# The second group's x times w_a, w_b and w_in with seven block products in place of eight

## The chip, the core and the metric

The kernel runs on one core of a Trainium2 chip. TensorE (PE in the profile; PEld is its loading of weights) multiplies, VectorE (DVE), ScalarE (ACT) and GpSimd (POOL) do the rest on rows of up to 448 columns, SyncE (SP) issues the DMAs. TensorE alone writes products into PSUM, eight banks of 512 float32 columns; VectorE and ScalarE read them there, GpSimd works on SBUF only. The metric is the device time of one execution in microseconds, lower is better.

## What is computed

Attention with normalised q and k over 4 batches of 12 heads (448 tokens, 64 columns a head), then two feed-forward layers on the 1792 tokens of 768 columns. Cut to what matters:

```python
def rmsnorm(x, g):
    return x / np.sqrt(np.mean(x * x, axis=-1, keepdims=True) + 1e-06) * g
scores = scale * np.matmul(rmsnorm(q, g_q), rmsnorm(k, g_k).transpose(0, 1, 3, 2))
attn = np.exp(scores - np.max(scores, axis=-1, keepdims=True))
attn = attn / (np.sum(attn, axis=-1, keepdims=True) + 1e-09)
x = np.matmul(attn, v)                              # to (1792, 768)
x = ((x @ w_a) * (x @ w_b)) @ w_out                 # w_a, w_b: 768 x 1536
h = x @ w_in                                        # 768 x 2048
out = (h * np.clip(h + 3.0, 0.0, 6.0) / 6.0) @ w_out2
```

## The kernel before

Tokens stand in columns. A batch has 448, so one matmul has 448 columns and 128x128 of weights. Every operand of the feed-forward layers lies as two float32r parts, a high one (rounded by ScalarE) and a low one (the rest, by a subtraction on VectorE or GpSimd, `sub`, line 342), and a product is three matmuls: high x high, high x low, low x high (`tri`, lines 627 to 629).

The batches form two groups of two (`GB`). Attention of all four batches comes first in due time; the first group's layers run beside the attention of the later batches, and the second group's layers after that. The `layer` calls at lines 786 to 790 are: first layer for batch 0, for batch 1, second layer for both; then first and second layer for the second group. A weight piece is 128 rows of a product, 768 wide: it is converted once from the stored 64-bit form (`convert`) and kept in DRAM, and each later use loads it (`wf`), rounds it whole on ScalarE (line 612) and makes the low part in two halves of 384 columns (`piece`). In the second group the low parts are VectorE's alone (`no_pool`).

In a layer, `unit` makes 128 rows of x times w_b, w_a or w_in for one batch in one PSUM bank, 18 matmuls. VectorE gates (`up_a`, `up_i`), and the result is split into `act`. `down` takes two rows of chunks (`SLICE`) and adds w_out's product to `acc`: for each of 6 blocks of 128 output rows and each batch a bank with six matmuls, called a unit of `down` below, then an addition on VectorE (line 721). After the last `down` of the first layer `acc` is the next layer's x and is split into `xx` (`to_x2`, line 735); the second group's first x comes from attention in `xf` and is split by `next_x` while the first group's last `down` runs.

What stands where on each engine is decided beforehand: `Plan.run` takes every operation with its due time, its cost by engine and its needs, goes through time on paper, lets each free engine take the most urgent operation whose data and buffers are there, and emits the instructions in that order. The costs written at the operations (378 for two matmuls of scores, 1135 for six of a unit, 567 for three of `down`) and the due times (`T` for the heads of each batch, `R` for each layer pass) set the order. On the chip each engine works through its own row, and waits where an operand isn't there. PSUM banks and SBUF buffers are `Slot`s which `Buf`s take in turn, the first free one of a list.

## Time and profile before

| | |
|---|---|
| median of 3 runs | 1321.78 us (1321.41 to 1322.69) |
| profiled execution: span from the first to the last instruction | 1319.6 us |
| TensorE busy | 99% of the span |
| VectorE, ScalarE, GpSimd busy | 68%, 46%, 13% |

The profiled execution has no time of its own beside the span; the median of the runs is 2.2 us above it. A busy share tells how much of the span an engine worked, not whether it was waited for; the chain of waits follows the last instruction back to what released it each time. Busy shares by stretch show where the engines' loads differ: attention and the first group until some 810 us, the second group's layers alone from 820 us on. In rows of single instructions, start and duration are in us, and what ended an idle time stands in brackets. Matmuls overlap: one takes 0.37 us, and the next begins 0.2 us after it.

### The profile page before, as it was taken

The numbers are of one execution on the slowest core, as the hardware profiler recorded it, in microseconds if no ns is written. First come the engines' busy times: TensorE is split into PE (matmuls) and PEld (weight loads), VectorE is DVE, ScalarE is ACT, GpSimd is POOL, SyncE is SP. The second block draws the span as 40 slices with busy tenths as digits, with TensorE's granted clock in tenths as the row PEclk, the third lists the DMA queues.
The fourth block names the chain that finished last, engine by engine and source line by source line (L and its number), as shares of the span: only waits on it lengthen the run. The fifth ranks groups of instructions, "written<-read, shape, count | busy, mean of one in ns | idle before, by whom it ended". The sixth has DMA issues, their size and how long they took to land.

```text
span 1319.6 us, 17987 instructions
## 1 busy us (share of the span) xinstructions
PE 1302.0 (99%) x6648; PEld 1097.5 (83%) x6648; DVE 891.3 (68%) x1648; ACT 609.6 (46%) x1249; POOL 171.5 (13%) x228
## 2 busy tenths in 40 slices
PE   5999999999999999999999999999999999999998
PEld 3668888888888888888887887999999999999997
DVE  8998999876576898877778654445444454555554
ACT  6886767675244566547556652111111143222220
POOL 3423222330010220111111012000000030000000
PEclk8999999999999999999999999999999999999999
DMA  6446776664332554444334113221111111111102
GB/s 210 162 142 230 246 253 226 216 216 131 97 104 89 162 178 159 160 163 143 99 137 164 45 44 113 61 60 48 59 50 60 48 52 58 48 60 48 61 24 84
DMA packets 52361, 155.32 MB, mean 118 GB/s; under 512 B 5936, under 2 KB 18608, under 8 KB 52272
## 3 DMA queue, kind: packets, MB, share of 16 engines
q1 hardware_dynamic: 52272, 154.16, 35.4%
q8 instruction: 52, 0.85, 0.3%
q14 instruction: 37, 0.30, 0.1%
HBM read 121.90 MB, written 32.24 MB: 117 GB/s over the span
## 4 chain that ended last, share of the span: by engine, by line
PE 98%; DVE 1%; ACT 0%; DMA 0%; SPq 0%; issue 0%; POOL 0%; DVEq 0%; ACTq 0%
PE bank L627 26%; PE bank L629 25%; PE bank L628 25%; PE bank L543 7%; PE bank L516 5%; PE bank L478 3%; PE bank L479 3%; PE bank L443 1%; PE bank L530 1%; PE bank L532 1%; PE bank L554 0%; PE bank L533 0%; DMA gg<-in_g_dram 0%; ACT p L488 0%; DVE rn L430 0%
## 5 line engine op out<-in xcount | busy, mean ns | idle before, releaser
L627 PE MATMUL bank<-xx,w 128*128 128x448 f32 x960 | 359.1, 374 | 0.0
L629 PE MATMUL bank<-xx,w 128*128 128x448 f32 x960 | 352.3, 367 | 0.0
L628 PE MATMUL bank<-xx,w 128*128 128x448 f32 x960 | 352.2, 367 | 0.0
L612 ACT ACTIVATE w<-wf 128x768 fp32r<-128x768 f32 x172 | 141.8, 842 | 338.2 <-PE bank L628 329.8
L627 PE MATMUL bank<-act,w 128*128 128x448 f32 x672 | 252.0, 375 | 0.0
L721 DVE TENSOR_TENSOR acc<-bank,acc 128x448 f32<-128x448 f32 x264 | 164.3, 623 | 122.1 <-PE bank L629 120.1
L629 PE MATMUL bank<-act,w 128*128 128x448 f32 x672 | 246.7, 367 | 0.0
L628 PE MATMUL bank<-act,w 128*128 128x448 f32 x672 | 246.6, 367 | 0.0
L627 PEld LDWEIGHTS bank<-xx,w 128*128 128x128 f32 x960 | 180.3, 188 | 19.6 <-issue 1.4
L629 PEld LDWEIGHTS bank<-xx,w 128*128 128x128 f32 x960 | 180.2, 188 | 16.9
L628 PEld LDWEIGHTS bank<-xx,w 128*128 128x128 f32 x960 | 180.5, 188 | 15.5
L342 DVE TENSOR_TENSOR w<-wf,w 128x384 fp32r<-128x384 f32 x283 | 148.4, 567 | 37.4 <-ACT w L612 33.2
L627 PEld LDWEIGHTS bank<-act,w 128*128 128x128 f32 x672 | 126.2, 188 | 16.7 <-DVE acc L721 2.4
L629 PEld LDWEIGHTS bank<-act,w 128*128 128x128 f32 x672 | 126.2, 188 | 12.0
L628 PEld LDWEIGHTS bank<-act,w 128*128 128x128 f32 x672 | 126.3, 188 | 10.9
L484 DVE TENSOR_REDUCE nm<-bank 128x1 f32<-128x448 f32 x168 | 102.3, 619 | 29.4 <-PE bank L479 24.0
L353 ACT ACTIVATE pt<-bank 128x512 f32<-128x512 f32 (+1 forms) x127 | 69.5, 550 | 98.9 <-PE bank L516 92.0
L488 ACT ACTIVATE p<-bank,nm,rstd 128x448 f32<-128x448 f32 x133 | 95.6, 721 | 29.5 <-PE bank L532 20.4
L342 POOL TENSOR_TENSOR w<-wf,w 128x384 fp32r<-128x384 f32 x61 | 65.5, 1087 | 290.7 <-ACT w L612 266.4
L670 ACT ACTIVATE act<-bank 128x448 fp32r<-128x448 f32 x112 | 60.8, 543 | 87.5 <-DVE bank L688 43.9
L543 PE MATMUL bank<-pt,rv 128*64 128x448 f32 (+1 forms) x384 | 93.3, 567 | 0.0
L342 DVE TENSOR_TENSOR act<-bank,act 128x448 fp32r<-128x448 f32 x112 | 69.5, 621 | 29.2 <-ACT act L670 28.7
(93 smaller groups left out, 1393.7 us busy)
## 6 DMA issues: line engine op xcount, KB each, us to landing
wst<-in_w_dram SPq DMA_DIRECT2D x68, 768.0 KB, 5.0
wf<-kept SPq DMA_DIRECT2D x104, 384.0 KB, 3.1
kept<-wf SPq DMA_DIRECT2D x68, 384.0 KB, 2.6
rq<-in_qt_dram SPq DMA_DIRECT2D x48, 224.0 KB, 2.8
rn<-in_nat_dram SPq DMA_DIRECT2D x23, 448.0 KB, 3.8
rv<-in_nat_dram SPq DMA_DIRECT2D x24, 224.0 KB, 2.6
out_dram<-acc SPq DMA_DIRECT2D x24, 224.0 KB, 1.9
rn<-in_nat_dram SPq DMA_DIRECT2D x2, 128.0 KB, 2.1
```

What stands on the lines that cost most here:

```text
L342: e.tensor_tensor(out=out, in0=a, in1=b, op=ALU.subtract)
L353: A.activation(out, in_, AF.Copy)
L484: add(at(u + OC[1]), {"V": 531}, lambda e, s=s, nm=nm: e.tensor_reduce(out=nm.t, in_=s.t[:, :S], axis=AX.X, op=ALU.max, negate=True), read ...
L488: add(at(u + OC[3]), {"A": 704}, lambda e, j=j, s=s, nm=nm, p=p: e.activation(p.t, s.t[:, :S], AF.Exp, bias=nm.t, scale=rstd.t[:, qcol[j]: ...
L516: e.transpose(t.t[:, c * P:(c + 1) * P], ps[4 * i + c].t[:, k * P:(k + 1) * P], ident)
L543: e.matmul(pv.t[rows, :S], rv.t[own[i], at_v[i]], pt.t[own[i], cols[i]:cols[i] + S], start=k == 0, stop=k == 3)
L612: add(due - LEAD + OW[2], {"A": on_act(DM)}, lambda e: e.activation(w.t[:, 0], wf.t.bitcast(F32), AF.Copy), reads=both, writes=[(w, 0, 0), ...
L627: e.matmul(ps, w.t[:, 0, wsl], xh, start=start, stop=False)
L628: e.matmul(ps, w.t[:, 0, wsl], xl, start=False, stop=False)
L629: e.matmul(ps, w.t[:, 1, wsl], xh, start=False, stop=stop)
L670: add(due, {"A": 424}, lambda e: e.activation(a.t[:, 0], ps.t[:, :S], AF.Copy), reads=[ps], writes=[(a, 0)])
L721: add(due, {"V": 535}, lambda e, m=m, bi=bi, ps=ps: e.tensor_tensor(out=acc[:, m, bi], in0=ps.t[:, :S], in1=acc[:, m, bi], op=ALU.add), re ...
```

## The change

In the second group, x times w_a, w_b and w_in is done by pairs of weight pieces. A pair (256 rows of the product, 768 deep) is cut into four blocks of 128 rows by 384, and x into four: the upper and the lower three chunks of its depth, for either batch. The four blocks of the result come from seven block products in place of eight (Strassen's scheme in Winograd's form). Each product is nine matmuls into one bank. Four run into the same bank `a`, one into `d`, two into `c`; between them VectorE or ScalarE takes the bank's content so far out (`t1`, `u2`, `t5`), and VectorE adds what makes the blocks `c11`, `c22`, `c12`; the fourth stays in `a` (`quads`, `STEPS`, `after`).

The right operands are x's blocks and sums: `b11`, `b21`, `b22`, `t1` in `xx`, and `t2`, `t3`, `t4` in `xt` (`x_maker`): 4 subtractions and 7 splits for each of three chunks, in place of 4 splits. They are made as the last units of the layer before come out of TensorE, in the order `XORDER`, with lines 389 (subtraction) and 692 and 851 (high parts). The left operands are three of the four blocks of the weights and four sums of them (`left_operands`, `ws`, line 902), each split as a half of 384 columns (`halve`, line 882 and 389), and GpSimd may do a part of all these subtractions. Evictions are at lines 404 and 946, the gate at 972, the new `down` at 999 to 1010.

`xt`, `ws`, `wb` and `tmpx` lie where attention's tiles lay: the pool is opened (`switch`) after attention's last operation. For that, batch 3's heads are due earlier (`T`), and the costs of TensorE's operations are 206.7 ns a matmul now (`MM`). The first group's layers compute as before.

```diff
-T = (6.793, 78.0, 255.0, 476.984)
+T = (6.793, 78.0, 255.0, 440.0)
-R = ((85.0, 1.515), (255.0, 1.267), (411.278, 1.34), (703.581, 0.977), (955.373, 0.615))
+R = ((85.0, 1.515), (255.0, 1.267), (411.278, 1.34), (703.581, 1.0), (950.0, 1.0))
...
+MM = 206.7
+LW7 = (34.0, 25.0, 20.0, 18.0)
...
+    FIRST = (("rn", 2, [P, 14, D], F32), ("rq", 2, [P, S], F32), ("rv", 2, [P, NCK, D], F32), ("sq", 1, [P, 14, D], F32),
+             ("kc", 1, [P, NCK, 2, D], F32R), *((k, 1, [P, 4 * P], F32R) for k in ("qh0", "qh1", "ql0", "ql1")),
+             ("kk", 2, [P, S], F32R), ("p", 7, [P, S], F32), ("pt", 2, [P, 2 * S], F32))
+    SECOND = (("xt", 9, [P, 2, S], F32R), ("wb", 2, [P, 2, PH], F32R), ("ws", 6, [P, PH], F32), ("tmpx", 3, [P, S], F32))
...
+    def switch(e):
+        pools[0].__exit__(None, None, None)
+        pool = ctx.enter_context(pools[1])
+        for k, ss, shape, dt in second:
+            for i, s in enumerate(ss):
+                s.tile, s.busy = pool.tile(shape, dt, name=f"{k}{i}"), False
...
-            add(at(u + OC[0]), {"PE": 378 * len(mine)}, score, reads=["zeros", *(x[i] for x in (qhs, qls, kks) for i in mine)], writes=[s])
+            add(at(u + OC[0]), {"PE": 2 * MM * len(mine)}, score, reads=["zeros", *(x[i] for x in (qhs, qls, kks) for i in mine)], writes=[s])
...
-            add(at(u + OD[1]), {"PE": 778}, value, reads=[(pt, 0), (pt, 1), rv], writes=[pv])
+            add(at(u + OD[1]), {"PE": 930}, value, reads=[(pt, 0), (pt, 1), rv], writes=[pv])
...
-                add(due, {"PE": 1135}, go, writes=[ps], reads=[
+                add(due, {"PE": 6 * MM}, go, writes=[ps], reads=[
...
+            if bi == 0 or m >= HX:
+                own({(0, 0): "b11", (1, 0): "b21", (1, 1): "b22"}[m // HX, bi], m, bi)
+            all4 = [(n, i) for n in (j, j + HX) for i in range(GB)]
+            if not there.issuperset(all4):
+                return
+            (k11, k12, k21, k22), (x11, x12, x21, x22) = zip(*((key(*x), src[:, x[0], x[1]]) for x in all4))
+            vg = {"V": (535, True), "G": on_pool(S)}
+            t3 = buf("tmpx")
+            def minus(after_us, out, x, y, reads, writes, after=()):
+                add(due + after_us, vg, lambda e: sub(e, out(), x, y), reads=reads, writes=writes, after=after)
+            minus(0.3, lambda: t3.t, x22, x12, [k12, k22], [t3], after)
+            minus(0.2, lambda: x12, x12, x11, [k11, *hold(all4[1])], [k12])
+            own("t1", j, 1)
+            minus(0.4, lambda: x22, x22, x12, [k12, *hold(all4[3])], [k22])
+            minus(0.6, lambda: x21, x21, x22, [k22, *hold(all4[2])], [k21])
+            for name, x, reads in (("t2", lambda: x22, [k22, *hold(all4[3])]), ("t3", lambda: t3.t, [t3]),
+                                   ("t4", lambda: x21, [k21, *hold(all4[2])])):
+                w = buf("xt")
+                out = [(w, 0), (w, 1)]
+                add(due + 0.8, {"A": 467}, lambda e, w=w, x=x: e.activation(w.t[:, 0], x(), AF.Copy),
+                    reads=reads, writes=out[:1], after=after)
+                add(due + 1.8, vg, lambda e, w=w, x=x: sub(e, w.t[:, 1], x(), f32(w.t[:, 0])),
+                    reads=[*reads, out[0]], writes=out[1:])
+                sevens[name, j] = (lambda w=w: (w.t[:, 0], w.t[:, 1])), out
...
+        def halve(src, keys, due, lo):
+            w = buf("wb", "w")
+            add(due - LW7[2], {"A": on_act(PH)}, lambda e: e.activation(w.t[:, 0], src(), AF.Copy),
+                reads=keys, writes=[(w, 0)], after=ends)
+            add(due - LW7[3], lo, lambda e: sub(e, w.t[:, 1], src(), f32(w.t[:, 0])),
+                reads=[*keys, (w, 0)], writes=[(w, 1)])
+            return w
...
+            s = {k: buf("ws") for k in (1, 3, 2, 4)}
+            sums = {k: (lambda k=k: s[k].t, [s[k]]) for k in s}
+            for k, x, y, op in ((1, a[1, 0], a[1, 1], ALU.add), (3, a[0, 0], a[1, 0], ALU.subtract),
+                                (2, sums[1], a[0, 0], ALU.subtract), (4, a[0, 1], sums[2], ALU.subtract)):
+                add(due - LW7[1] + 0.2 * k, gv, lambda e, k=k, x=x, y=y, op=op: e.tensor_tensor(
+                    out=s[k].t, in0=x[0](), in1=y[0](), op=op), reads=[*x[1], *y[1]], writes=[s[k]], after=ends)
+            return a[0, 0], a[0, 1], sums[2], sums[1], sums[3], sums[4], a[1, 1]
...
+        STEPS = (("a", "b11", True), ("d", "b21", True), ("a", "t2", False), ("c", "t1", True), ("a", "t3", False),
+                 ("c", "b22", False), ("a", "t4", False))
...
+            turns = [(0, k) for k in range(7)] if len(todo) == 1 else [
+                (0, 0), (0, 1), (1, 0), (1, 1), (0, 3), (0, 2), (0, 5), (0, 4), (1, 3), (0, 6), (1, 2), (1, 5), (1, 4), (1, 6)]
+            dues = {t: clock(9 * MM) for t in turns}
+            left = [left_operands(*x, dues[q, 0]) for q, x in enumerate(todo)]
+            ps, t = [{} for _ in todo], [{} for _ in todo]
+            after = {0: ("t1", "a", None), 1: ("c11", "d", "t1"), 2: ("u2", "a", None), 3: ("t5", "c", None),
+                     4: ("c22", "a", "t5"), 5: ("c12", "c", "u2")}
...
+                def go(e, to=to, w=w, xs=xs, first=first):
+                    out = to.t[:, :S]
+                    for j, (x, _) in enumerate(xs):
+                        hi, lo = x()
+                        for a, x, n in ((0, hi, 0), (0, lo, 1), (1, hi, 2)):
+                            e.matmul(out, w.t[:, a, chunk(j)], x, start=first and j + n == 0,
+                                     stop=j + n == HX + 1, skip_group_check=not first)
+                add(dues[q, k], {"PE": 9 * MM}, go, writes=[to],
+                    reads=[(w, 0), (w, 1), *(key for _, keys in xs for key in keys)])
+                if k not in after:
+                    continue
+                due = dues[q, k] + 9 * MM * 1e-3
+                new, name, other = after[k]
+                t[q][new], from_ = buf("tmpx"), ps[q][name]
+                if other is None:
+                    add(due, {"A": 424, "V": 535}, lambda e, o=t[q][new], x=from_: copy(e, o.t, x.t[:, :S]),
+                        reads=[from_], writes=[t[q][new]])
+                else:
+                    add(due, {"V": 535}, lambda e, o=t[q][new], x=from_, y=t[q][other]: e.tensor_tensor(
+                        out=o.t, in0=x.t[:, :S], in1=y.t, op=ALU.add), reads=[from_, t[q][other]], writes=[t[q][new]])
...
+        if no:
+            for i, got in enumerate(quads([("i", 0), ("i", 1)])):
+                finished(i, got)
+        else:
+            got = quads([("b", 0), ("a", 0)])
+            finished(0, got[1], kept_b(got[0]))
+        for i in range(1 + no, n):
+            bs = None if no else kept_b(quads([("b", i)])[0])
+            if no == 0 and i < n - 1:
+                down(i - 1)
+            finished(i, quads([(ups[-1], i)])[0], bs)
+            if no:
+                down(i - 2)
...
-    layer(0, 0, (0,), BM[0], pace(*R[0]), SLICE[0])
-    layer(0, 0, (1,), BM[1], pace(*R[1]), SLICE[1])
-    layer(1, 0, (0, 1), BM[2], pace(*R[2]), SLICE[2], True)
-    layer(0, 1, (0, 1), BM[3], pace(*R[3]), SLICE[3])
-    layer(1, 1, (0, 1), BM[4], pace(*R[4]), SLICE[4])
+    layer(0, (0,), BM[0], pace(*R[0]), SLICE[0], LF[0])
+    layer(0, (1,), BM[1], pace(*R[1]), SLICE[1], LF[0])
+    ends[:] = [add(690.0, {"G": (1, False)}, switch, after=ends)]
+    first_x = x_maker(xf, lambda m, bi: ("xf", m, bi), 0.0, ends, held)
+    layer(1, (0, 1), BM[2], pace(*R[2]), SLICE[2], LF[2], lambda k, due: first_x(XORDER[k], due))
+    layer7(0, BM[3], pace(*R[3]), LF[2], x_maker(acc, lambda m, bi: ("acc", m, bi), 15.0))
+    layer7(1, BM[4], pace(*R[4]), LF[3], lambda mb, due: put(mb[0], GB + mb[1], due))
```

TensorE at the place where the second layer of the second group begins (`act` is the gated product, `w` and `wb` are weights, `xx` and `xt` are x). Before:

```order
L628 MATMUL bank1_64<-act1_197,w1_193 128x448
L629 MATMUL bank1_64<-act1_197,w1_193 128x448
L627 MATMUL bank1_64<-act3_199,w2_194 128x448
L628 MATMUL bank1_64<-act3_199,w2_194 128x448
L629 MATMUL bank1_64<-act3_199,w2_194 128x448
L627 MATMUL bank0_63<-xx_143,w3_195 128x448
L628 MATMUL bank0_63<-xx_143,w3_195 128x448
```

Now:

```order
L999 MATMUL bank0_63<-act5_178,w1_170 128x448
L1000 MATMUL bank0_63<-act5_178,w1_170 128x448
L1001 MATMUL bank0_63<-act5_178,w1_170 128x448
L932 MATMUL bank0_63<-xx_143,w2_171 128x448 x9
L932 MATMUL bank1_64<-xx_143,w1_170 128x448 x9
L932 MATMUL bank2_65<-xx_143,w3_172 128x448 x9
L932 MATMUL bank3_66<-xx_143,w3_172 128x448 x9
L932 MATMUL bank4_67<-xx_143,w2_171 128x448 x9
L932 MATMUL bank0_63<-xt0_6639,wb0_6648 128x448 x3
```

The last unit went to bank 1 and the next product began in bank 0; now the last unit fills bank 0, and the first of the new products goes to bank 0 again, with its neighbours in banks 1 to 4.

VectorE at the same place (`acc` is the running sum, and x of the second layer). Before:

```order
L721 TENSOR_TENSOR acc_145<-bank0_63,acc_145 128x448
L721 TENSOR_TENSOR acc_145<-bank1_64,acc_145 128x448
L342 TENSOR_TENSOR w0_192<-wf0_189,w0_192 128x384
L342 TENSOR_TENSOR xx_143<-acc_145,xx_143 128x448
L342 TENSOR_TENSOR w1_193<-wf1_190,w1_193 128x384 x2
L342 TENSOR_TENSOR w2_194<-wf2_191,w2_194 128x384 x2
L688 SCALAR_TENSOR_TENSOR bank0_63<-tmp0_202,bank0_63 128x448
L342 TENSOR_TENSOR act0_196<-bank0_63,act0_196 128x448
L342 TENSOR_TENSOR w3_195<-wf0_189,w3_195 128x384 x2
```

Now:

```order
L1010 TENSOR_TENSOR acc_145<-bank0_63,acc_145 128x448
L389 TENSOR_TENSOR acc_145<-acc_145 128x448
L389 TENSOR_TENSOR xx_143<-acc_145,xx_143 128x448
L389 TENSOR_TENSOR acc_145<-acc_145 128x448
L389 TENSOR_TENSOR xx_143<-acc_145,xx_143 128x448
L389 TENSOR_TENSOR acc_145<-acc_145 128x448
L389 TENSOR_TENSOR xt3_6642<-acc_145,xt3_6642 128x448
L389 TENSOR_TENSOR xt4_6643<-tmp0_179,xt4_6643 128x448
L389 TENSOR_TENSOR xt5_6644<-acc_145,xt5_6644 128x448
L389 TENSOR_TENSOR xx_143<-acc_145,xx_143 128x448
L389 TENSOR_TENSOR tmp0_179<-acc_145 128x448
L389 TENSOR_TENSOR xx_143<-acc_145,xx_143 128x448
```

Behind the last addition one split of x stood among splits of weights; now twelve operations on x stand in a row, which turn `acc` into t1, t2 and t4 in place and make the low parts.

VectorE inside the first layer of the second group, where the products with w_a are gated. Before:

```order
L678 TENSOR_TENSOR bank0_63<-bank0_63,tmp0_202 128x448
L342 TENSOR_TENSOR act0_196<-bank0_63,act0_196 128x448
L678 TENSOR_TENSOR bank1_64<-bank1_64,tmp1_203 128x448
L342 TENSOR_TENSOR w2_194<-wf1_190,w2_194 128x384 x2
L342 TENSOR_TENSOR act1_197<-bank1_64,act1_197 128x448
L357 COPY tmp0_202<-bank0_63 128x448
L357 COPY tmp1_203<-bank1_64 128x448
L342 TENSOR_TENSOR w3_195<-wf2_191,w3_195 128x384 x2
```

Now:

```order
L404 COPY tmpx2_6658<-bank0_63 128x448
L902 TENSOR_TENSOR ws4_6654<-wst0_164,ws3_6653 128x384
L946 TENSOR_TENSOR xf_144<-bank1_64,tmpx2_6658 128x448
L972 TENSOR_TENSOR tmp0_179<-xf_144,tmp0_179 128x448
L404 COPY tmpx2_6658<-bank0_63 128x448
L389 TENSOR_TENSOR act0_173<-tmp0_179,act0_173 128x448
L404 COPY xf_144<-bank1_64 128x448
L946 TENSOR_TENSOR tmp0_179<-bank0_63,xf_144 128x448
L389 TENSOR_TENSOR w3_172<-wf1_167,w3_172 128x384
L972 TENSOR_TENSOR tmpx1_6657<-tmp0_179,tmpx1_6657 128x448
L946 TENSOR_TENSOR tmp0_179<-bank1_64,tmpx2_6658 128x448
L389 TENSOR_TENSOR w2_171<-wf1_167,w2_171 128x384
```

Two gates out of PSUM were followed by copies of w_b's products; now the banks of the seven products are emptied one by one (404, 946), with sums of weights (902), gates (972) and halves of weights between.

## Rows read from the trace of the kernel before

**Rows 1.** The page: span, and busy us (share of the span) xinstructions of the engines.

```profile
span 1319.6 us, 17987 instructions
PE 1302.0 (99%) x6648; PEld 1097.5 (83%) x6648; DVE 891.3 (68%) x1648; ACT 609.6 (46%) x1249; POOL 171.5 (13%) x228
```

**Rows 2.** The page: chain that ended last, share of the span by engine.

```profile
PE 98%; DVE 1%; ACT 0%; DMA 0%; SPq 0%; issue 0%; POOL 0%; DVEq 0%; ACTq 0%
```

**Rows 3.** Busy us (xinstructions) by stretch: PE, PEld, DVE, ACT, POOL; clock, DMA, GB/s.

```profile
30.00:812.00 782.00, 781.59 (x4155) 629.55 (x4154) 617.48 (x1154) 479.17 (x1030) 148.05 (x199) 1.00 0.47 156
820.00:1315.00 495.00, 495.00 (x2397) 449.62 (x2396) 246.61 (x427) 110.58 (x168) 13.80 (x12) 1.00 0.17 53
```

**Rows 4.** What TensorE waited for: us, times, longest us; whole span, then from 30 us.

```profile
PE bank L443 <- DVE kc L342: 9.3, 2, 8.3
...
PE bank L478 <- ACT p L488: 0.4, 1, 0.4
```

**Rows 5.** Single instructions where the second layer begins: start us, us, engine, line, operation.

```profile
1066.88 12.33 POOL L342 TENSOR_TENSOR xx<-acc,xx 128x448 fp32r<-128x448 f32 x10
...
1067.98 0.63 DVE L721 TENSOR_TENSOR acc<-bank,acc 128x448 f32<-128x448 f32 x1 [0.61 <-PE bank L629]
...
1077.50 0.37 PE L629 MATMUL bank<-act,w 128*128 128x448 f32 x1
1077.70 0.37 PE L627 MATMUL bank<-xx,w 128*128 128x448 f32 x1
...
1078.44 1.17 DVE L342 TENSOR_TENSOR w<-wf,w 128x384 fp32r<-128x384 f32 x1
...
1078.62 0.58 ACT L728 ACTIVATE xx<-acc 128x448 fp32r<-128x448 f32 x1
```

**Rows 6.** The same view, VectorE alone: instructions that stand ready one after another.

```profile
1064.26 0.62 DVE L721 TENSOR_TENSOR acc<-bank,acc 128x448 f32<-128x448 f32 x1
1064.80 0.61 DVE L342 TENSOR_TENSOR act<-bank,act 128x448 fp32r<-128x448 f32 x1
...
1080.08 1.95 DVE L342 TENSOR_TENSOR w<-wf,w 128x384 fp32r<-128x384 f32 x4
```

**Rows 7.** Line 342, subtractions, whole span: ns min/median/max, first and last start us, forms.

```profile
L342 DVE TENSOR_TENSOR w<-wf,w x283: 544/553/1362, 107.5 to 1294.7; 128x384 fp32r<-128x384 f32 x142
...
L342 POOL TENSOR_TENSOR w<-wf,w x61: 997/1017/1623, 25.9 to 779.1; 128x384 fp32r<-128x384 f32 x61
...
L342 POOL TENSOR_TENSOR xx<-acc,xx x17: 1148/1160/1695, 286.3 to 1078.0; 128x448 fp32r<-128x448 f32 x17
...
L342 DVE TENSOR_TENSOR xx<-xf,xx x3: 627/1582/1593, 781.4 to 796.5; 128x448 fp32r<-128x448 f32 x3
```

**Rows 8.** ScalarE's groups, 820 to 1320 us: xcount | busy us, mean ns | idle before.

```profile
L612 ACT ACTIVATE w<-wf 128x768 fp32r<-128x768 f32 x64 | 52.9, 843 | 253.6 <-PE bank L628 253.6
...
L728 ACT ACTIVATE xx<-acc 128x448 fp32r<-128x448 f32 x12 | 6.9, 579 | 7.4 <-DVE acc L721 7.4
```

**Rows 9.** TensorE's first matmuls, and the stretch they lie in (eighth figure: granted clock).

```profile
22.32 0.86 PE L443 MATMUL bank<-identr,kc 64*128 64x64 f32 x4 [1.55 <-POOL kc L342]
...
25.57 0.57 PE L478 MATMUL bank<-kk,qh 128*128 128x448 f32 x1
25.95 0.57 PE L479 MATMUL bank<-kk,ql 128*128 128x448 f32 x1
...
20.00:30.00 10.00, 8.02 (x35) 5.25 (x33) 9.97 (x22) 8.51 (x24) 4.84 (x8) 0.66 0.61 210
```

**Rows 10.** VectorE's subtractions for weights, 30 to 812 us, grouped.

```profile
L342 DVE TENSOR_TENSOR w<-wf,w 128x384 fp32r<-128x384 f32 x155 | 82.9, 574 | 8.2 <-ACT w L612 6.1
```

200 lines of the change are left out of this document (166 added, 34 removed).

## The prediction

> **What bounds the kernel now.** I read the page's busy shares first, then its chain of waits, then the busy time by stretches, and last single instructions where the change acts. TensorE is busy 1302.0 of 1319.6 us, VectorE 68%, ScalarE 46%, GpSimd 13% [rows 1], and 98% of the chain that ended last is TensorE's own work [rows 2]. By stretches it is stricter: from 30 to 812 us TensorE is busy 781.59 of 782 us, from 820 to 1315 us all 495 [rows 3]. The one real wait is 8.3 us at the start; after 30 us one of 0.4 us is left [rows 4]. So a matmul less is time less, and any new wait of TensorE is time more. In the second stretch 2397 matmuls take 495.00 us, 0.2065 us each [rows 3]. VectorE works 247 of those 495 us, ScalarE 111, GpSimd 14: there is room beside TensorE, but the work put there has due moments.
>
> **What is removed.** A pair of weight pieces (256 rows of the product) took eight block products of nine matmuls (three chunks, three split parts) over the two batches and takes seven. There are 6 pairs of w_a, 6 of w_b, 8 of w_in: 20 x 9 = 180 matmuls fewer, 2268 in the second group instead of 2448. 180 x 0.2065 = **37.2 us**. Against the profiled execution: span 1319.6 - 37.2 = 1282.4 us. The median of the runs, 1321.78, is 2.2 us above that span; I carry the 2.2 over and get 1284.6 us before anything is charged.
>
> What that price rests on: the new products have the same forms (128x128 weights, 448 columns), and loads of weights still come one per matmul. The page "TensorE: Matmul & The Clock Gate" of the Trainium skill (section "Wait — 56ns, not 53.3ns?") gives columns divided by 2.4 GHz plus 2.5 ns, an estimate of 189 ns for 448 columns. By it the gain would be 34.1 us and the sum 1287.7; the row's 0.2065 is what this kernel's pattern takes, so it is used.
>
> **What is added on average.** VectorE gets about 650 instructions for the second group instead of 460. When they stand ready they start 0.54 us apart for 448 columns, though one takes 0.62, and 0.47 for 384, (1.95 - 0.55) / 3 [rows 6]: 650 x 0.54 = 350 us at most of some 470, 75%. From 30 to 812 us it is busy 617 of 782, 79%, and TensorE doesn't wait there [rows 3]. ScalarE goes to about 313 instructions, by the order, nearly all of 384 or 448 columns, at 0.58 us or less [rows 8]: 180 us of 470. Neither becomes the bound on average. Loads of weights and stores are as many as before, into other tiles; no queue gets more. Hence the cost of the change is where TensorE meets an operand that is late. There are four such places.
>
> **1. The first 812 us: 0.** The same instructions, in another order, since the plan now charges TensorE 206.7 ns a matmul (189 before) and batch 3's heads are due 37 us earlier. Their end moves ahead of the second group: 110 matmuls (22.7 us) lie between the last product with v and the group's first product, where the two overlapped before. Nothing in the rows gives this a sign. Bounds: -3 (of the 8.3 us wait and the slow clock after it, rows 4 and 9) and +5 (the second rival).
>
> **2. x is made for the first layer: 1.5 us.** Before, 24 instructions split twelve blocks of x. Now t1, t2, t3, t4 are formed too: 21 splits and 12 subtractions, beside 12 additions of the last units, halves of weights and their sums. TensorE has 72 matmuls of units, 14.9 us, after it has read the old x for the last time. VectorE's part from the first low half of x to the low half that closes the second product's x (block 5 of batch 0) is 35 instructions, 18 us at 0.47 to 0.54 [rows 6], plus some 4 us, an estimate, in which it waits for ScalarE's high halves and activations, 0.58 to 0.63 us each [rows 5, 8]. It can begin 17.5 us ahead, when ScalarE has its first high half, and ends about 4.5 us behind the first product's due start. On the way unit 3 needs bank 0, whose addition for unit 1 stands behind the last gate of the old products: 1 us. TensorE, so much later, wants the low half at 4.1: 0.4 more. I take 1.5. Bounds 0 (VectorE never waits) and 4.
>
> **3. x is made for the second layer: 4.5 us.** This is the tight place, for x comes out of the last units themselves. Take 0 as the end of the twelfth unit; a unit of six matmuls takes 1.24 us. The sum of unit 4 is in acc at -9.2 (unit end, plus 0.04 and 0.63, rows 5). With it VectorE makes the first third of the operands, by the order ten instructions, unit 5's addition among them, ahead of the rows shown: 5.4 us, and about 0.6 of waiting or meeting GpSimd: -3.2. Only then come the additions of units 6 to 12, seven on the row, 3.8 us: done at 0.6, or 1.0 since unit 12's can't begin before 0. The order gives the first product bank 0, the one unit 12 has just filled: TensorE waits until about **1.2**. In the trace of before the same hand-over has no gap: the old unit went to bank 1, the next to bank 0, 1077.50 to 1077.70 us [rows 5]. The first product then runs to 3.1. Its neighbour (b21) wants the low half of block 5 after six matmuls, at 4.3; on VectorE that is the ninth instruction behind the additions, the last but two of the order rows, and some 1.4 us of waits lie among them (0.2 for a difference that GpSimd makes in 1.16 us, 0.6 in meeting it, rows 7; 0.6 for a high half on ScalarE, rows 5): 1.0 + 9 x 0.54 + 1.4 = 7.3. Wait **3.0**. From there TensorE is late enough: t1's last low half, six instructions on, is there at 10.6, and is wanted at 12.8. Sum 4.2, and 0.3 for further meetings with GpSimd: 4.5. Bounds: 1.2 (only the bank), and 8: 4.5 and the 3.4 us that the lower clock cost once, when TensorE stood for 1.55 us at 20.8 us: granted 0.66 in 20 to 30 us, that is 6.8 us at 1.2 GHz, with matmuls 0.37 us apart [rows 9].
>
> **4. Hand-overs in between: 3 us.** A product's bank must be emptied before TensorE comes back to it, one product (1.86 us) or unit (1.24 us) later. There are 20 x 7 evictions of products and 14 x 12 of units, 308 in all; the third piece of the order shows how halves and sums stand between them. For a unit an addition of 0.63 us leaves 0.2 to 0.4 us [rows 5]; the old kernel had this and no gap. What can eat it is GpSimd: it gets 91 instructions in the second group, 20 before, and VectorE's with two operands in SBUF rise from 140 to 349. A weight half on VectorE has median 553 ns and maximum 1362, x from xf 627 and 1593 [rows 7]; at 1078.44 one took 1.17 us beside GpSimd, while additions from PSUM in the same stretch kept 0.63 [rows 5]. So meetings cost 0.6 to 0.9 us. How often: between 30 and 812 us weight halves lost 155 x (574 - 553 ns) = 3.3 us [rows 7, 10] and two x halves 1.9, 5 us for 148 us of GpSimd [rows 3]. 91 x 1.06 us = 96 us of it in the second group makes 3.4 us of VectorE lost; I take 3, as if most reached TensorE. Bounds 0 and 10.
>
> **Sum.** 1284.6 + 0 + 1.5 + 4.5 + 3 = **1293.6 us**; the ends of all four together are 1282.8 and 1311.6.
>
> **Rivals.**
> - *All is covered.* GpSimd and ScalarE at their medians, x ready in time; only bank 0 costs its 1.2 us: 1285 to 1288. For it: TensorE's row without a gap from 30 us on. Against it: place 3 is tight by the order alone.
> - *The first group loses a cushion.* The old plan charged TensorE 189 ns for what takes 206.5, so in the trace the other engines run ahead of their plan; with 206.7 that lead is gone, and their lateness shows. Price: the 5 us that VectorE loses there to GpSimd, if all reaches TensorE, up to three times that if ScalarE and the weights' conversion join: 1299 to 1310. For it: VectorE at 79% there. Against it: rows hold no wait that the lead would have to cover.
> - *GpSimd holds VectorE up at every turn, and it is slower than before.* Place: the second group's products and units. Price: 91 instructions, each with one VectorE instruction held 0.62 us, is 56 us: 1284.6 + 6 + 56 = 1347. It decides from (37.2 - 6) / 91 = 0.34 us a GpSimd instruction; half of it gives 1319. Against it: 0.035 us lost per us of GpSimd in the first group, where the plan keeps the two apart as it does here.
>
> The page "SBUF — State Buffer" of the Trainium skill (section "Who interferes with whom") makes that last case a rule: a VectorE instruction with two SBUF inputs and a GpSimd one that reads SBUF take the shared port pair one after the other, and the second blocks until the first is done. The trace agrees in size, 553 against 1362 ns, and with PSUM additions unharmed, 0.63; how often it happens here the rule doesn't tell.
>
> **How the numbers follow.** Forecast, 1288 to 1300: 0.55. All covered: 0.15. Cushion lost, 1299 to 1310: 0.18. GpSimd in the way: 0.07 for 1300 to 1319, 0.05 beyond. The change not doing what it says has no chance of its own: the order has 180 matmuls fewer. The range 1284 to 1306 leaves out the upper part of the cushion case and the GpSimd case, some 0.17. Within 0.2% (2.6 us, what a measurement of this kernel can tell) of 1321.8 lies 0.02 of the last case, 0.05 beyond it; faster is 0.93.
>
> **What would show it.** Right: 2268 matmuls at 0.2065 us in the second group, TensorE busy but for a gap of 1 to 1.5 and one of 2 to 4 us where the second layer's x is made, VectorE near 75% there. Place 3 is wrong if neither gap stands at its first two products; place 4 if acc or the evictions release TensorE for more than 10 us in total; the zero for place 1 if the second group's first product starts later than 816 us. The sum falls if the matmul pace in the second group isn't 0.206, or if VectorE instructions over 1 us stand there by the dozen.

## The result, and where the time went

The changed kernel takes 1294.35 us (median of four runs, 1293.22 to 1294.67), the kernel before 1322.24 us beside it; the ratio is 0.9786, 95% interval 0.9772 to 0.9800. The sum forecast, 1293.6, is within a microsecond. Its terms are not: two effects that I had at nothing are worth +5.5 and -7.4 us, and that they nearly cancel is luck. The profiled execution has a time of 1294.45 us and a span of 1292.7.

The page of the changed kernel, its span, the engines' busy time and the chain that ended last, as in [rows 1] and [rows 2]:

```profile
span 1292.7 us, 18152 instructions
PE 1261.6 (98%) x6468; PEld 1060.6 (82%) x6468; DVE 1021.3 (79%) x1853; ACT 671.0 (52%) x1440; POOL 230.6 (18%) x262
...
PE 83%; DVE 10%; DMA 3%; ACT 2%; issue 1%; SPq 0%; POOL 0%; DVEq 0%; ACTq 0%
```

TensorE lost 180 instructions and is still the bound, but its share of the chain fell from 98% to 83%, and VectorE's rose from 1% to 10%: TensorE bounds the time less strictly. How much less is read from two stretches that hold the same work: from the moment at which the second group's matmuls are all that is left, to the end. The columns are those of [rows 3] (a count takes in matmuls that cross an edge, here two). The kernel before, whose second group has 2448 matmuls and begins among the first group's last ones, and the changed one, with 2268 from 817.07 us on:

```profile
809.80:1319.60 509.80, 506.14 (x2449) 458.56 (x2447) 248.87 (x430) 111.75 (x170) 13.92 (x12) 1.00 0.17 55
```

```profile
817.00:1292.70 475.70, 465.42 (x2270) 423.54 (x2268) 362.23 (x616) 166.23 (x328) 97.27 (x81) 1.00 0.18 57
```

So the first part became 817.0 - 809.8 = 7.2 us **longer**, and the second part 509.8 - 475.7 = 34.1 us shorter, 26.9 together. Of the second part, 180 matmuls at 0.2067 us are 37.2. TensorE stands 475.70 - 465.42 = 10.3 us there in place of 3.7 (before, all of it behind the last matmul): 6.6 given back. That leaves -3.5, which no wait explains: the matmuls themselves follow one another faster. Before, by their start times in the trace, all intervals from 819 us on are 206 or 207 ns. Now most come in a round of five (199, 207, 202, 203 and 202 ns, 202.7 on average): some 1820 of 2220 intervals without a disturbance, four fifths. The slow pace is left for some 400, nearly all between 912 and 994 us. A stretch of each (a count takes in up to two matmuls that cross an edge):

```profile
836.00:893.00 57.00, 57.00 (x283) 52.87 (x282) 44.69 (x72) 19.19 (x38) 15.66 (x15) 1.00 0.21 66
955.00:989.00 34.00, 34.00 (x166) 30.90 (x165) 25.76 (x42) 10.28 (x20) 9.77 (x9) 1.00 0.20 58
```

That saves 7.4 us; 3.9 of it go in late loads of weights and in starts after a stand.

What TensorE waited for from 30 us on, in the view of [rows 4] (there 0.4 us in all):

```profile
PE bank L932 <- ACT tmp L400: 3.4, 3, 2.1
PE bank L525 <- ACT p L535: 2.2, 2, 1.3
PE bank L932 <- DVE xx L389: 1.9, 2, 1.7
PE bank L675 <- DVE acc L781: 1.7, 2, 1.1
PE bank L932 <- DVE acc L1010: 0.9, 1, 0.9
...
PE bank L999 <- DVE acc L1010: 0.3, 1, 0.3
...
```

Where the second layer's x is made (the place of [rows 5]), single instructions, in order of time:

```profile
1060.50 3.80 DVE L1010 TENSOR_TENSOR acc<-bank,acc 128x448 f32<-128x448 f32 x7
...
1063.20 0.36 PE L1001 MATMUL bank<-act,w 128*128 128x448 f32 x1
...
1064.22 1.43 DVE L389 TENSOR_TENSOR acc<-acc 128x448 f32<-128x448 f32 x1
...
1064.44 3.89 PE L932 MATMUL bank<-xx,w 128*128 128x448 f32 x16 [0.88 <-DVE acc L1010]
...
1069.32 0.61 DVE L389 TENSOR_TENSOR xx<-acc,xx 128x448 fp32r<-128x448 f32 x1
...
1069.99 6.15 PE L932 MATMUL bank<-xx,w 128*128 128x448 f32 x29 [1.65 <-DVE xx L389]
```

Seven additions in a row end at 1064.30; the first product, in the bank that the last unit filled, starts 0.88 us late; the second product (b21) stops after seven matmuls until VectorE has the low half that it wants, 1.65 us. Both gaps stand where the prediction put them, at 0.88 and 1.65 for 1.2 and 3.0. A third, 0.88 us at 1080.66, is their echo: an eviction on ScalarE comes late behind one on VectorE.

Where the first layer's x is made, VectorE is busy without a pause from 809 to 834 us. Stretches of the changed kernel:

```profile
795.00:812.00 17.00, 16.35 (x80) 14.41 (x78) 14.71 (x24) 9.33 (x19) 11.25 (x10) 1.00 0.34 119
812.00:833.00 21.00, 17.66 (x84) 14.92 (x82) 21.00 (x38) 10.12 (x22) 6.96 (x5) 1.00 0.37 122
833.00:1060.00 227.00, 226.73 (x1109) 207.52 (x1110) 173.16 (x285) 68.74 (x134) 58.98 (x53) 1.00 0.20 60
...
1110.00:1285.00 175.00, 174.99 (x861) 160.46 (x860) 124.77 (x219) 58.01 (x114) 13.95 (x12) 1.00 0.14 46
```

TensorE stands 0.65 + 3.34 us in the first two stretches, and 0.27 and 0.01 in the long ones. The longest of these stands, 2.08 us, ends at 833.00; its chain, single instructions:

```profile
831.70 0.61 DVE L946 TENSOR_TENSOR tmp<-bank,tmp 128x448 f32<-128x448 f32 x1
...
832.40 0.54 ACT L400 ACTIVATE tmp<-bank 128x448 f32<-128x448 f32 x1 [2.93 <-DVE tmp L946]
...
833.00 0.47 PE L932 MATMUL bank<-xx,w 128*128 128x448 f32 x1 [2.08 <-ACT tmp L400]
```

The bank is emptied by ScalarE, which had stood 2.93 us for a buffer that VectorE had still to read; VectorE came to it only after eight operations on x and on weights, in a row from 826.92 us on. The wait bears ScalarE's name and is VectorE's lateness.

### The profile page after: what moved, and what is told of

It is laid out like the page before. It is cut to its first block, busy times and chain, and to the rows that moved or that the text cites. A ratio compares the mean times of both kernels' runs of the same rounds, so it can differ in the third digit from the quotient of the medians.

```text
span 1292.7 us, 18152 instructions
## 1 busy us (share of the span) xinstructions
PE 1261.6 (98%) x6468; PEld 1060.6 (82%) x6468; DVE 1021.3 (79%) x1853; ACT 671.0 (52%) x1440; POOL 230.6 (18%) x262
## 4 chain that ended last, share of the span: by engine, by line
PE 83%; DVE 10%; DMA 3%; ACT 2%; issue 1%; SPq 0%; POOL 0%; DVEq 0%; ACTq 0%
PE bank L932 17%; PE bank L675 11%; PE bank L676 11%; PE bank L677 11%; PE bank L590 5%; PE bank L999 5%; PE bank L1000 5%; PE bank L1001 5%; PE bank L563 4%; PE bank L525 3%; PE bank L526 3%; DMA wst<-in_w_dram 1%; PE bank L490 1%; DMA rn<-in_nat_dram 1%; DVE xx L389 1%
## 5 line engine op out<-in xcount | busy, mean ns | idle before, releaser
L675 PE MATMUL bank<-xx,w 128*128 128x448 f32 x480 | 182.2, 380 | 0.6 <-DVE act L389 0.3
L677 PE MATMUL bank<-xx,w 128*128 128x448 f32 x480 | 175.5, 366 | 0.0
L676 PE MATMUL bank<-xx,w 128*128 128x448 f32 x480 | 175.5, 366 | 0.0
L932 PE MATMUL bank<-xx,w 128*128 128x448 f32 x567 | 124.8, 367 | 5.8 <-ACT tmp L400 3.0
L675 PE MATMUL bank<-act,w 128*128 128x448 f32 x336 | 128.0, 381 | 1.7 <-DVE acc L781 1.7
L660 ACT ACTIVATE w<-wf 128x768 fp32r<-128x768 f32 x104 | 85.4, 839 | 81.5 <-PE bank L676 61.5
L389 DVE TENSOR_TENSOR w<-wf,w 128x384 fp32r<-128x384 f32 x198 | 111.8, 600 | 16.1 <-ACT w L660 12.1
L677 PE MATMUL bank<-act,w 128*128 128x448 f32 x336 | 122.9, 366 | 0.0
L676 PE MATMUL bank<-act,w 128*128 128x448 f32 x336 | 122.9, 366 | 0.0
L932 PEld LDWEIGHTS bank<-xx,w 128*128 128x128 f32 x567 | 106.0, 188 | 17.0 <-ACT tmp L400 3.7
L389 POOL TENSOR_TENSOR w<-wf,w 128x384 fp32r<-128x384 f32 x56 | 60.7, 1095 | 287.6 <-ACT w L660 241.9
L999 PE MATMUL bank<-act,w 128*128 128x448 f32 x276 | 101.6, 368 | 0.0
L1000 PE MATMUL bank<-act,w 128*128 128x448 f32 x276 | 101.2, 366 | 0.0
L1001 PE MATMUL bank<-act,w 128*128 128x448 f32 x276 | 101.0, 366 | 0.0
L675 PEld LDWEIGHTS bank<-xx,w 128*128 128x128 f32 x480 | 90.3, 188 | 12.2 <-issue 2.1
L677 PEld LDWEIGHTS bank<-xx,w 128*128 128x128 f32 x480 | 90.2, 188 | 7.5
L932 PE MATMUL bank<-xt,w 128*128 128x448 f32 x432 | 95.4, 366 | 0.4 <-ACT tmp L400 0.4
```

What stands on the lines that cost most here:

```text
L389: e.tensor_tensor(out=out, in0=a, in1=b, op=ALU.subtract)
L660: add(due - LEAD + OW[2], {"A": on_act(DM)}, lambda e: e.activation(w.t[:, 0], wf.t.bitcast(F32), AF.Copy), reads=both, writes=[(w, 0, 0), ...
L675: e.matmul(ps, w.t[:, 0, wsl], xh, start=start, stop=False)
L676: e.matmul(ps, w.t[:, 0, wsl], xl, start=False, stop=False)
L677: e.matmul(ps, w.t[:, 1, wsl], xh, start=False, stop=stop)
L932: e.matmul(out, w.t[:, a, chunk(j)], x, start=first and j + n == 0, stop=j + n == HX + 1, skip_group_check=not first)
```

## Experiments: the plan's charges, and the first group

The changed kernel charges TensorE 206.7 ns a matmul in its plan, 189 before. First that alone in the kernel before, then the reverse.

```diff
-            add(at(u + OC[0]), {"PE": 378 * len(mine)}, score, ...
+            add(at(u + OC[0]), {"PE": 413.4 * len(mine)}, score, ...
...
-                add(due, {"PE": 1135}, go, writes=[ps], reads=[
+                add(due, {"PE": 1240.2}, go, writes=[ps], reads=[
```

> The kernel before, in which only the plan's charges for TensorE are those of the changed kernel: 206.7 ns a matmul in place of 189 (413.4 for 378, 1240.2 for 1135, 620.1 for 567, 930 for 778). Due times, pools and products stay. Theory (the new charges take a lead of VectorE and ScalarE away, and that is where the changed kernel's first group became 7 us longer): 1326 to 1331 us, and TensorE's waits between 30 and 812 us grow from 0.4 to some 4 us. Rival (the earlier heads of batch 3 or the two pools did it): within 1.5 us of 1322, waits as before.

1329.12 us, ratio 1.0043 (1.0028 to 1.0058): that is 5.7 us more, by charges on paper alone. TensorE's waits from 30 to 812 us:

```profile
PE bank L627 <- DVE act L342: 2.4, 2, 1.9
PE bank L478 <- ACT p L488: 2.2, 2, 1.3
...
```

5.1 us with the two shorter ones, for 0.4 [rows 4]. The profiled execution's span is 1327.6 us, 8.0 longer; the other 3.3 us stand in no wait of this view. That the charges did it is shown; why is argued: with 189 ns the plan believes that TensorE is sooner at everything than it is, so the other engines' rows are laid out to be early; with 206.7 they are just in time on paper, and late on the chip wherever an instruction takes longer than its charge.

> The changed kernel, with the old charges (378, 778, 1135, 567) for attention and the first group's layers alone; the second group keeps 206.7 ns. Theory (the charges lengthened the first group): the second group's first product starts at 810 us in place of 817, and the time is 1286 to 1290 us. Rival (due times or pools): first product at 816 to 818, 1293 to 1296 us.

1292.45 us (0.9775, 0.9758 to 0.9791). The first product starts at 811.26, 5.8 us earlier, as the theory said; the time is only 1.9 us less (1.5 by the ratios, whose intervals overlap). TensorE, and the stretch around it:

```profile
811.26 1.61 PE L932 MATMUL bank<-xx,w 128*128 128x448 f32 x7
817.88 1.49 PE L932 MATMUL bank<-xx,w 128*128 128x448 f32 x3 [5.02 <-DVE xx L389]
```

```profile
812.00:821.00 9.00, 3.98 (x14) 3.23 (x13) 9.00 (x19) 3.32 (x7) 4.16 (x2) 0.81 0.16 56
```

After seven matmuls TensorE stands 5.02 us for x, and the granted clock is 0.81 on average there. The charges cost the changed kernel's first group some 6 us, but taking them back gives little: the place behind it, where x is made, takes up most of it.

## Experiments: VectorE where the first x is made

> The changed kernel with the old charges for attention and the first group (the run a_oldcosts), and with the making of the second group's first x due 6 us earlier, so that VectorE's row takes it between the additions of the first group's last units. In a_oldcosts the first group ended 5.8 us earlier, but TensorE then stood 5.2 us at the first products, while VectorE had waited 0.6 us ahead of each of ten additions a little before. Theory (x's operations merely stood behind those additions): the 5.2 us fall to 1 or less and the time is 1286 to 1289 us. Rival (x cannot be made sooner, since attention's last outputs and VectorE's load set its end): a gap of 4 to 5 us stays, 1291 to 1294 us.

```diff
-    first_x = x_maker(xf, lambda m, bi: ("xf", m, bi), 0.0, ends, held)
+    first_x = x_maker(xf, lambda m, bi: ("xf", m, bi), 6.0, ends, held)
```

1299.16 us, slower than a_oldcosts by 6.7. TensorE's wait for x is gone, and it stands for the first group instead: 7.2 us for additions into `acc` (line 781) and 3.7 for `act`, with a granted clock of 0.80 from 800 to 826 us.

> The changed kernel with its own charges, and only the making of the second group's first x due 6 us earlier. Theory (VectorE's crowded 25 us around 820 us are what TensorE waits for there): the waits between 795 and 834 us, 4.0 us together, fall to about 1 us, 1290 to 1292 us. Rival (the waits come from elsewhere, or wander to the additions that are now later): 1293.5 to 1295 us.

1296.36 us, 2.0 more than the changed kernel (0.9799, 0.9784 to 0.9813: not clear of the noise): the waits for additions rose from 1.7 to 4.3 us. Both runs missed on the same side. In both orders what is put last is late, which fits a VectorE that hasn't the time in these 25 us. Next, more time, by heads of batch 3 that are due 10 us earlier (`T` ends in 430.0).

> The changed kernel with the old charges for attention and the first group (a_oldcosts) and batch 3's heads due 10 us earlier still (430 in place of 440), so that 174 matmuls in place of 108 lie between attention's last product and the second group's first one. a_oldcosts and a_old_x6 showed that VectorE, busy without a pause from 809 us on, cannot make x, the first weights and the last additions in the 23 us it has there, in whatever order. Theory (room for it is what is missing): the first product starts at 811 to 813 us and waits less than 1.5 us, no stretch at the lower clock there, 1286.5 to 1289.5 us. Rival (attention squeezed into less time costs what it gives): 1291 to 1295.

1293.86 us (0.9784, 0.9767 to 0.9800); and the same due time with the new charges:

> The changed kernel with its own charges and batch 3's heads due 10 us earlier (430 in place of 440): 174 matmuls in place of 108 between attention's last product and the second group's first. Theory (room for VectorE ahead of the second group): the waits between 795 and 834 us, 4.0 us together, fall to 1.5 or less, 1290.5 to 1292.5 us. Rival (attention's part gets longer by as much): 1294 to 1297.

1300.54 us (0.9830, 0.9816 to 0.9845). Both missed, and both have one stand of 8.4 us. In a_old_t430 VectorE, ScalarE and TensorE:

```profile
798.36 0.61 DVE L389 TENSOR_TENSOR xt<-tmp,xt 128x448 fp32r<-128x448 f32 x1
...
799.01 0.63 ACT L746 ACTIVATE tmp<-bank,half_c 128x448 f32<-128x448 f32 x1 [1.90 <-DVE xt L389]
...
801.80 0.74 PE L675 MATMUL bank<-act,w 128*128 128x448 f32 x1 [8.36 <-DVE act L389]
```

Earlier heads let x's difference t3 take one of the two buffers `tmp` before the gate of the first group's last unit (line 746) got it; x waited for VectorE, the gate for the buffer, TensorE for the gate. The last run gives t3 buffers of its own and 5 us of lead to x.

```diff
-    K["tmpx"][:0] = K["tmp"]
+    K["t3"], K["tmpx"] = list(K["tmpx"]), K["tmp"] + K["tmpx"]
...
-            t3 = buf("tmpx")
+            t3 = buf("t3")
```

> The run a_old_t430 (the changed kernel with the old charges for attention and the first group, and batch 3's heads due at 430) with two edits. The difference t3 of x no longer takes one of the two buffers tmp, which the gates of the first group's last units need, and the making of the second group's first x is due 5 us earlier. In a_old_t430 TensorE stood 8.4 us at 793 to 802 us, and 10.2 us there were at the lower clock: ScalarE's first step of the gate could not begin before VectorE had read t3 out of that buffer, at 798.9 us. Theory (the stand came from the shared buffer, not from VectorE's load): it goes, and with it the lower clock, 8.4 and some 2.8 us; up to 2 us come back where x is made: 1283 to 1286 us, 1294.35 for the changed kernel. Rival (VectorE's load sets the end of that place, and another wait takes the stand's place): 1290 to 1294 us.

1294.23 us (0.9785, 0.9772 to 0.9798): the stand of 8.4 us is gone, and the time is the changed kernel's all the same. The run changes two things at once; that the shared buffer held up the gate rests on the rows above. Two waits took the stand's place, single instructions of TensorE and, ahead of the first, VectorE:

```profile
799.53 1.44 DVE L389 TENSOR_TENSOR xt<-xf,xt 128x448 fp32r<-128x448 f32 x1
800.89 1.56 DVE L389 TENSOR_TENSOR xt<-tmpx,xt 128x448 fp32r<-128x448 f32 x1
802.38 1.54 DVE L389 TENSOR_TENSOR xt<-xf,xt 128x448 fp32r<-128x448 f32 x1
...
804.51 0.47 PE L675 MATMUL bank<-act,w 128*128 128x448 f32 x1 [2.91 <-DVE acc L781]
...
1095.82 1.39 PE L932 MATMUL bank<-xt,w 128*128 128x448 f32 x4 [2.76 <-DVE xf L404]
```

Three low parts took 1.44 to 1.56 us in place of 0.61, beside GpSimd, and the additions behind them came late. Here hold-ups by GpSimd did reach TensorE. By the starts of the same matmuls the profiled execution is 5.1 us ahead of the changed kernel's at 795 us of the latter, 5.7 at 834 and 6.1 at 1092: in this execution the crowded place no longer eats what the first group saved. The second wait, in the second layer, came with the lower clock and took back 3.3 us of it. This execution, 1291.67 us, was the fastest of the five; why the others lost more isn't known. No run of this chapter is clearly faster than the changed kernel.

## Experiments: the bank and GpSimd

> The changed kernel, with the eight PSUM banks of the second layer of the second group listed from the other end, so that its first product no longer gets the bank that the last unit of the first layer has just filled. Theory (x's last low half sets the moment from which TensorE can go on; the bank's wait lies inside that): the gap of 1.0 us ahead of the first product goes and the one of 1.8 us ahead of the second product's last matmuls grows by as much; the time stays within 0.5 us. Rival (each gap adds): 1.0 us less, the second gap as before.

```diff
-BM = ((0, 2, 3, 4), (7, 1), (0, 1, 7), ALLB, ALLB)
+BM = ((0, 2, 3, 4), (7, 1), (0, 1, 7), ALLB, ALLB[::-1])
```

1293.41 us (one run). The first product now starts without a gap, and stops for x instead, after seven of its nine matmuls:

```profile
1062.19 0.37 PE L1001 MATMUL bank<-act,w 128*128 128x448 f32 x1
1062.40 1.58 PE L932 MATMUL bank<-xx,w 128*128 128x448 f32 x7
...
1065.26 2.11 PE L932 MATMUL bank<-xx,w 128*128 128x448 f32 x9 [1.28 <-DVE xx L389]
1069.01 6.14 PE L932 MATMUL bank<-xx,w 128*128 128x448 f32 x29 [1.64 <-DVE xx L389]
```

The gap ahead of the second product's last matmuls stayed, 1.64 us, where the theory had it grow; the new one, 1.28 us, is for the last low half of the first product's own x (b11). In the changed kernel that low half is late by some 0.4 us, too little for its views to name a wait. So TensorE stands 2.9 us, 2.53 in the changed kernel with its two named gaps, and it passes the place with the same lead on the changed kernel that it had ahead of it, 1.0 us. The time at the place follows VectorE's row of x, as the theory said, and the bank's wait lay inside it.

> The changed kernel, with GpSimd taken out of the second group: x's subtractions, sums and low halves of weights, gates and low parts of act are VectorE's alone. In the changed kernel VectorE's instructions there were held up 49 times, 28 us in all, where GpSimd worked. Theory (hardly any of that reaches TensorE, since VectorE has time to spare; what GpSimd takes off VectorE at the two places where x is made is worth more): VectorE's hold-ups vanish, TensorE's waits at the two places grow by 2 to 4 us, and the time is 1295 to 1299 us. Rival (the hold-ups were what cost TensorE its waits outside these places): 1290 to 1293 us.

```diff
-        vg, gv = {"V": (on_dve(PH), True), "G": on_pool(PH)}, {"G": on_pool(PH), "V": (on_dve(PH), True)}
+        vg = gv = {"V": (on_dve(PH), True)}
```

(and the same at x's subtractions, the gate and the low parts of `act`). 1299.50 us, 5.1 more (0.9816, 0.9793 to 0.9839: 4.0 by the ratios, whose intervals just overlap). TensorE's waits from 795 us on:

```profile
PE bank L932 <- ACT xx L692: 4.8, 1, 4.8
PE bank L675 <- DVE acc L781: 4.8, 4, 2.8
PE bank L999 <- DVE acc L1010: 0.4, 1, 0.4
...
```

None of VectorE's instructions is held up now, and TensorE's waits from 795 us on are 2.4 us longer than in the changed kernel. A good part of the rest came with the clock: behind the stands of 2.79 and 4.83 us it was 0.79 from 818 to 826 us and 0.83 from 1060 to 1080 us, where the changed kernel had 1.00. So GpSimd's help where x is made is worth more than its meetings cost, as expected, in part by the clock, and the time is half a microsecond above the range. In the changed kernel 49 of VectorE's instructions from 795 to 1290 us took over 0.06 us more than the faster ones of their form, 28 us in all (17.6 of it from 833 to 1060 us), and in that long stretch TensorE stood 0.27 us.

## Experiments: two paces of the same matmuls

> The kernel before, with one extra matmul of 64 columns (identity by identity, into the unused columns of the bank) ahead of ten of the second group's units; nothing else is changed. Before, matmuls of 448 columns follow one another 206.7 ns apart from 818 us to the end; in the changed kernel two thirds of them follow 202.7 ns apart, and the switches from one to the other come right at a load of weights that is some 0.07 to 0.12 us late. Theory (the two paces are two ways in which loads and matmuls can fall into step, and any small disturbance chooses anew): most of the 2400 matmuls after 820 us go 202.7 ns apart, up to 9.6 us less, 1313 to 1318 us although work is added. Rival (the pace follows from what the matmuls read or from what runs beside them): 206.7 ns stay, and ten extra matmuls cost 1 to 2 us, 1322 to 1325.

```diff
+                    if g == 1 and j == 0 and bi == 0 and f % 3 == 0:
+                        e.matmul(ps.t[:, S:], identr, identr[:, :D], start=True, stop=True)
                     for x in (j, j + 1):
```

1322.68 us, no change (0.9997, 0.9988 to 1.0007). An extra matmul without a wait doesn't do it: the fast pace held for 246 intervals, from 818 to 868 us, until the second of them, and from there the slow one for some 2140. (The expectation's "two thirds" counts single intervals near 202 ns; the round of five has one of 207 as well, so that it was four fifths.)

> The kernel before, in which TensorE is made to stand six times in the second group (two at some 820 to 850 us, two at some 930, one each at 1100 and 1210): VectorE copies 64 columns of the unit that has just ended, and the next unit begins with a matmul of 64 columns on that copy. The ten small matmuls of b_nudge, without a wait, gave the pace of 202.7 ns for 50 us after the first and 206.7 ns after the others. Theory (a stand of TensorE lets the loads of weights get ahead, and the faster pace follows until something disturbs it again): after each stand the matmuls come 202.7 ns apart; six stands cost 0.7 to 1.0 us each, and the pace gives back up to 9: 1317 to 1320 us. Rival (stands don't choose the pace): 206.7 ns stay, 1326 to 1329 us.

```diff
+                held = g == 1 and j == 0 and bi == 1 and f in ((1, 7), (2, 9))[no]
+                if held:
+                    add(due - 2, {"V": 130}, lambda e, x=prev[0]: e.tensor_copy(gt, x.t[:, :D]), reads=[prev[0]], writes=["gt"])
...
+                    if held:
+                        e.matmul(ps.t[:, S:], identr, gt, start=True, stop=True)
```

1324.42 us, 1.0019 (1.0006 to 1.0032): the six stands cost a little more than they gave back, and neither number was met. The ten runs spread from 1322.72 to 1329.59 us, the profiled one took 1328.08. The pace did change; stretches between the stands:

```profile
845.00:960.00 115.00, 115.00 (x569) 106.60 (x568) 55.17 (x96) 18.06 (x26) 0.00 (x0) 1.00 0.18 55
...
1099.00:1106.00 7.00, 6.28 (x24) 5.68 (x25) 1.25 (x3) 1.39 (x3) 0.00 (x0) 0.76 0.00 0
...
1110.00:1205.00 95.00, 95.00 (x470) 88.03 (x470) 52.00 (x90) 23.29 (x36) 0.00 (x0) 1.00 0.16 51
1220.00:1320.00 100.00, 100.00 (x486) 90.81 (x485) 53.08 (x92) 22.38 (x35) 0.00 (x0) 1.00 0.15 51
```

569 matmuls in 115 us (as many from 980 to 1095 us) and 470 in 95 are 0.202 us each, 486 in 100 are 0.206. The stands of 0.98 us (two) were followed by the fast pace, those of 0.32 us (two) by the slow one, and those of 1.7 us (two) by 3.4 us at 1.2 GHz (0.76 granted from 1099 to 1106 us) and then by the fast and by the slow one. So one stand of the good kind, alone:

> The kernel before with one stand of TensorE alone, the second one of b_gap (at some 840 us, a wait of 1.0 us for VectorE's copy of 64 columns and a matmul on it). In b_gap the matmuls after that stand followed 202.7 ns apart until the next stand; the stands of 1.7 us there brought the lower clock for 3.4 us, this one did not. Theory (which of the two paces TensorE keeps is chosen at a stand and then stays, whatever the work is): some 2295 matmuls at 202.7 in place of 206.7 ns give 9.2 us, the stand costs 1.3: 1313.5 to 1316 us, faster although it does more. Rival (the faster pace needs the stands again and again): 1318 to 1323.

```diff
-                held = g == 1 and j == 0 and bi == 1 and f in ((1, 7), (2, 9))[no]
+                held = g == 1 and no == 0 and kind == "a" and j == 0 and bi == 1 and f == 1
```

1314.06 us, ratio 0.9935 (0.9920 to 0.9950): the kernel before, with one wait, one copy and one useless matmul **more**, is 8.3 us faster. TensorE at the stand, and the rest of the second group:

```profile
835.31 0.37 PE L630 MATMUL bank<-xx,w 128*128 128x448 f32 x1
836.66 0.30 PE L661 MATMUL bank<-gt,identr 128*128 128x64 f32 x1 [0.98 <-DVE gt L656]
```

```profile
845.00:1300.00 455.00, 455.00 (x2247) 421.62 (x2246) 231.94 (x401) 104.96 (x160) 12.71 (x11) 1.00 0.17 52
```

2247 matmuls in 455 us, 0.2025 us each, where [rows 3] has 2397 in 495, 0.2065: the same instructions on the same data, at the same granted clock. In these traces the pace changes only at a disturbance, though not at each, and is kept until another one. Both paces stand in the kernel before, too: the same three lines as in [rows 3]'s second stretch, in the first group, 17 intervals in 3.44 us, 0.202 us each.

```profile
459.71 0.36 PE L627 MATMUL bank<-act,w 128*128 128x448 f32 x1
...
463.15 0.37 PE L629 MATMUL bank<-act,w 128*128 128x448 f32 x1
```

## Why the prediction was right in sum, point by point

- **What is removed: 37.2 us.** The count was right, 180 matmuls. The price, "the row's 0.2065 is what this kernel's pattern takes", was half right: it is one of two paces, and the old kernel happened to be in the slower one from 819 us to its end, where nothing disturbed it. The changed kernel has the faster one for four fifths of the second group, 7.4 us that I didn't have; it begins behind waits and late loads. The trace of before could have shown it: from 30 to 810 us some 1460 of its 2420 undisturbed intervals have the faster pace. The 189 ns that I worked out from the Trainium skill's page "TensorE: Matmul & The Clock Gate" (section "Wait — 56ns, not 53.3ns?") is below both paces; no run here shows it.
- **Place 1, the first 812 us: 0; 5.5 measured.** That is the 7.2 us by which the first part grew, less 1.7 us of waits that belong to place 2 (0.65 and 1.05 us ahead of 817 us), outside the bounds of -3 and +5. This is the step that failed, and the sign named for it came: the first product starts at 817.07, later than 816 us. I wrote that "nothing in the rows gives this a sign" and set the lost lead against the forecast as a rival, with 0.18; it isn't an alternative to the other places but happens beside them. b_costs shows it by itself, 5.7 us by its ratio, and a_oldcosts takes it away, 5.8 us. Of the 5.5, 2.0 are added idle time of TensorE in the first 30 us (busy 14.45 us there, 16.44 before); and the faster pace is at work here too (82% of the undisturbed intervals from 30 to 810 us, 60% before), so that without it the first part would be some 2 us longer still. The sign could have been argued: a plan that charges less than an operation takes keeps the others early, and the new one gives that up.
- **Place 2: 1.5; 4.0 measured** (0.65 + 1.05 + 0.20 + 2.08), the upper bound. Two of its waits I had: an addition behind the old gates, 0.65 us for 1, and the x that the second product wants, 0.20 for 0.4. What I left out stands between and behind them: a later addition, 1.05 us, that is late because VectorE makes x, and an eviction, 2.08 us, that is late because VectorE then makes more of x and sums of weights. The place was to be summed for VectorE as a whole: it is busy 21.00 of 21 us.
- **Place 3: 4.5; 3.4 measured.** The two gaps came at the matmuls named, 0.88 and 1.65 us for 1.2 and 3.0; the echo of 0.88 us wasn't named. The second was over-sized for two reasons: VectorE had the low half at 1069.93 us, 6.5 us behind the last unit's end for 7.3, since its waits on the way were some 0.8 us and not 1.4; and TensorE came to it 0.6 us later than I had it, after seven matmuls and not six and behind b11's late low half. a_banks says that the bank is not the bound of the place, but VectorE's row of x.
- **Place 4: 3; 0.7 in waits** (0.27 and 0.44), and some 3.9 us in starts after stands and late loads, which I hadn't thought of. The mechanism was off by far: I had VectorE lose 3.4 us to GpSimd and nearly all of it reach TensorE; from 795 us on it lost 28 us, 0.31 us for each of GpSimd's 91 instructions, just under the 0.34 that the third rival named as its turning point, and almost none of it reached TensorE outside the crowded places. The 5 us from which I carried the 3.4 over took in two forms of instruction only: over all forms VectorE lost some 18 us from 30 to 812 us of the kernel before, in 43 instructions, beside 198 of GpSimd. The rule of the Trainium skill's page "SBUF — State Buffer" (section "Who interferes with whom"), that one of the two is blocked until the other is done, agrees with the rows: 1.44 to 1.56 us in a_t3x5 for low parts that take 0.61. The rule's loss was there; the rival was wrong in that all of it would be TensorE's.
- **The sum.** 0 + 1.5 + 4.5 + 3 = 9.0 on top of 1284.6 were forecast. Measured are 5.5 + 4.0 + 3.4 + 0.7 + 3.9 - 7.4 = 10.1 by places, 37.2 - 26.9 = 10.3 by spans, and 1294.45 - 1284.6 = 9.9 by the profiled execution's own time, which lies 1.8 us above its span and not 2.2. These places say where the time went, not what each would give back: a_oldcosts shortens place 1 by 5.8 us, and place 2 takes most of it. Both signs by which the sum was to fall came: the pace isn't 0.206, and 37 of VectorE's instructions from 817 us on took over 1 us, one in the kernel before from 820 us on. The sum held all the same, by offsets that I hadn't foreseen. Without the faster pace of the second group the kernel would have come to some 1302 us: inside the range, above the forecast's own 1288 to 1300. (The chances disagree by 0.02: 0.05 in one sentence for what lies beyond 1319 us, 0.02 and 0.05 in the next.)

## What to carry to other kernels

Sum a crowded place for the engine that does the work there, with everything it owes to anyone, and not along the one operand that the change adds: where VectorE is full, earlier x makes later additions, and six other orders, charges and due times gave 1292 to 1301 us. Charges in a plan are not neutral: making them true cost the kernel before 5.7 us, most likely because the untrue ones gave the other engines a lead; undoing it in the changed kernel gave back only 1.9, for the next place was full. And a matmul's price, read from one undisturbed stretch, holds for that stretch: look whether other stretches of the same trace have another, as they had here.
